# Loading a weight matrix in four row groups per slice, so that its casts need no change of partition

## The chip, the cores and the metric

The kernel runs on one core of a Trainium2 chip. The metric is device time in microseconds (us), the median of the runs shown; lower is better. TensorE multiplies; VectorE (DVE), ScalarE (ACT) and GpSimd (POOL) work on tiles; SyncE (SP) issues most of the transfers, which 16 DMA engines carry out.

## The reference

A linear attention with cosine weights (8 batches, 8 heads, 576 positions, head size 64) feeds a two-layer network with 4608 tokens, model width 512 and inner width 2048:

```python
def phi(x, c, s):
    r = np.maximum(x, 0.0)
    return np.concatenate([r * c, r * s], axis=-1)
q_p, k_p = phi(q, cos_w, sin_w), phi(k, cos_w, sin_w)
kv = np.einsum('bhsf,bhsd->bhfd', k_p, v)
z = np.sum(k_p, axis=2)
num = np.einsum('bhsf,bhfd->bhsd', q_p, kv)
den = np.einsum('bhsf,bhf->bhs', q_p, z)[..., None] + 1e-06
x = (num / den).transpose(0, 2, 1, 3).reshape(B * S, H * D)
h = x @ w_in
g = h * (1.0 / (1.0 + np.exp(-beta * h)))
out = g @ w_out
```

Inputs and output are float32; the kernel multiplies in bfloat16.

## The kernel before, in words

The tokens are taken in nine chunks of 512. For each batch the kernel applies the relu to q and k (L193, L192), scales v by cosine and sine (L219, L217), forms kv (`kv_mm`, L276), the numerators and denominators (`num_mm`, L297), divides (L308 to L319), and turns the result so that the model dimension lies on the partitions (`x_turn_pe`, L356, or a transposing transfer, L367). A chunk then goes through w_in in 16 groups of four matmuls of 128x512 (`h_mm`, L386), each followed by the activation (L394), and through w_out (`o_mm`, L544, for the first chunk; later chunks use a scheme with fewer products, L511 and L621). The order on each engine is the order in which the program text issues the instructions; there is no scheduler behind it.

Heads are paired on the partitions in an order of their own: in the turned x, partition jj*64 + d of block (jp, g) holds dimension d of head jp*4 + jj*2 + g. The rows of w_in must stand in the same order. w_in is loaded in four slices of 512 columns. `load_w("in", i)` (L95 to L103) reads slice i into a float32 stage tile of 128 partitions x 4 x 512: partition q of block j holds row j*128 + q. `cast_win` (L105) then makes the bfloat16 tile `win[i]`, and since rows of the two halves of the partitions have to change places, it works on pieces of 64 partitions. For one (g, jj) it reads partitions g*64 onward and writes partitions jj*64 onward:

```python
o = win[i].rearrange("q (jp g) f -> q jp g f", g=2)[jj * HP : (jj + 1) * HP, jps, g, f0:f1]
a = stages["in", i].rearrange("q (jp jj) f -> q jp jj f", jj=2)[g * HP : (g + 1) * HP, jps, jj, f0:f1]
```

Slice 0 is loaded in two transfers of 512 KB, right behind the first batch's q, k and v; slices 1 to 3 in one transfer of 1 MB each. Slice 0 is cast in eight pieces of 64x512 (five on GpSimd, two on VectorE, one on ScalarE), slice 1 in eight pieces of 64x2x256 on VectorE, slices 2 and 3 likewise with two of the eight on GpSimd (L113 GpSimd, L115 VectorE, L111 ScalarE).

There are four stage tiles. The four slices of w_out (`load_w("out", i)`, L101) reuse those of w_in, so each of these transfers waits until the casts of the slice before it in its tile are done. Behind the second of them on SP's queue stand the next batch's v, k and q (L79). VectorE and ScalarE scale w_out on its way to bfloat16 (L123, L121). The program gives the transfers of SP and ScalarE eight semaphores in turn, so that a transfer waits until the eighth before it has landed.

The part of the program around the change runs in this order: kv and numerators of the first batch's two head groups, casts of slice 0, division and turning of the second group, `cast_halves(1)`, then the slots of the first chunk (0 to 3 on slice 0, 4 to 7 on slice 1, and so on; 16 to 31 for w_out). `rest()` is issued at slot 4: casts of slices 2 and 3, the loads of w_out and of batch 1, scaling of w_out and the preparation of batch 1. Slots 22 and 23 issue batch 1's kv (L276) and the turning of its q (L235).

Of the kernel before, what the change touches and what calls it, by code (L numbers as in the profile page):

```python
# [16 lines left out]
P = 128  # L17
# [5 lines left out]
def kernel(  # L23
# [14 lines left out]
    nc = tc.nc  # L38
# [5 lines left out]
    MI = DM // P  # L44
# [4 lines left out]
    HP = P // 2  # L49
# [33 lines left out]
    win = [const.tile([P, MI, 512], BF16, name=f"win{i}") for i in range(4)]  # L83
# [4 lines left out]
    T1, T2, T4 = (const.tile([P, JT // 2, HM], BF16, name=f"T{i}") for i in (1, 2, 4))  # L88
    T3 = B12
    S1, S2, S3, S4 = (const.tile([P, JT // 2, TCH // 2], BF16, name=f"S{i}") for i in (1, 2, 3, 4))  # L90
    w_in_v = moe_w_in.rearrange("(j p) f -> p j f", p=P)
    w_out_v = moe_w_out.rearrange("(j p) m -> p j m", p=P)
    stages = {}

    def load_w(kind, i, step=4):  # L95
        if (kind, i) not in stages:
            stages[kind, i] = stage.tile([P, 4, 512], FP32, name="w_stage", tag="w_stage")
        st = stages[kind, i]
        for a in range(0, 4, step):
            if kind == "out":  # L100
                nc.sync.dma_start(out=st[:, a : a + step], in_=w_out_v[:, 4 * i + a : 4 * i + a + step, :])  # L101
                continue
            nc.sync.dma_start(out=st[:, a : a + step], in_=w_in_v[:, a : a + step, i * 512 : (i + 1) * 512])  # L103

    def cast_win(i, gj, eng="dve", f0=0, f1=512, jps=slice(0, 2)):  # L105

        g, jj = gj
        o = win[i].rearrange("q (jp g) f -> q jp g f", g=2)[jj * HP : (jj + 1) * HP, jps, g, f0:f1]
        a = stages["in", i].rearrange("q (jp jj) f -> q jp jj f", jj=2)[g * HP : (g + 1) * HP, jps, jj, f0:f1]
        if eng == "act":  # L110
            nc.scalar.copy(o, a)  # L111
        elif eng == "pool":
            nc.gpsimd.tensor_copy(o, a)  # L113
        else:
            nc.vector.tensor_copy(o, a)  # L115
# [7 lines left out]
            nc.vector.tensor_scalar(wout[:, j, :], st[:, jj, :],  # L123
                                    scalar1=rbeta[:, j : j + 1], scalar2=None, op0=ALU.mult)

    GJ = [(0, 0), (0, 1), (1, 0), (1, 1)]

    load_raw(0, "q", 0, 2)
    load_raw(0, "q", 2, 4)
# [5 lines left out]
    load_raw(0, "k", 2, 3)  # L135
    load_raw(0, "k", 3, 4)
    load_w("in", 0, 2)


# [150 lines left out]
    def num_mm(b, n, jp, bank, slot):  # L290

        for cs in range(2):
            for jj in range(2):
                rows = slice(jj * HP, (jj + 1) * HP)
                for g in range(2):
                    cols = slice(g * HP, (g + 1) * HP)
                    nc.tensor.matmul(  # L297
                        ps[cols, bank + jj, slot * E : (slot + 1) * E],
                        lhsT=(qts[b % 2], qs_of(b))[cs][rows, jp, n, cols],
                        rhs=kv[rows, g, jp, cs, :],  # L300
                        start=(cs == 0), stop=(cs == 1))

    def x_rden(bank, slot, n0, n1, jps):

        w, m = len(jps), n1 - n0
        nv = ps[:, bank : bank + 2, slot * E : (slot + w * m) * E].rearrange("q j (i s e) -> q j i s e", s=w, e=E)
        den = small.tile([P, 2, m, w], FP32, name="den", tag=f"den{m}{w}")
        nc.vector.tensor_tensor(  # L308
            den, nv[:, :, :, :, D],
            eps9[:, n0:n1].unsqueeze(1).unsqueeze(3).to_broadcast([P, 2, m, w]), op=ALU.add)  # L310
        rden = small.tile([P, 2, m, w], FP32, name="rden", tag=f"rden{m}{w}")
        nc.vector.reciprocal(rden, den)  # L312
        return nv, rden, n0, jps
# [409 lines left out]
    for i in range(1, 4):  # L723
        load_w("in", i)
# [14 lines left out]
    for n in range(7):  # L739
        num_mm(0, n, 1, 0, n)  # L740
    num_mm(0, 7, 1, 6, 0)
    for gj, eng in zip(GJ, ("pool", "dve", "pool", "dve")):
        cast_win(0, gj, eng, jps=slice(0, 1))
    for gj, eng in zip(GJ, ("act", "pool", "pool", "pool")):
        cast_win(0, gj, eng, jps=slice(1, 2))
    got = x_rden(0, 0, 0, 7, (1,))
    x_mul_act(x_rden(6, 0, 7, 8, (1,)), 7)
    x_mul(got, 0, 4)
# [4 lines left out]
    x_turn_pe(0, 4, 8, 1, ("act",), (1,))  # L753
    h_mm(0, 3, (0, 1))

    def cast_halves(i, fs=(0, 256)):
        for f in fs:
            for gj in GJ:
                cast_win(i, gj, "pool" if i > 1 and gj == GJ[3] else "dve", f, f + 256)

    cast_halves(1)

    def rest():

        cast_halves(2)
        cast_halves(3)
        x_mul(x_rden(2, 0, 8, NQ, (0, 1)), 8, NQ)
        load_w("out", 0)
        load_w("out", 1)
        load_raw(1, "v")  # L770
        load_raw(1, "k")
        load_raw(1, "q")
        load_w("out", 2, 2)
        load_w("out", 3, 2)
        x_turn_dma(0, 8, 9)
        for j in range(8):
            cast_out(j)
        v_scale(1, 0)
        v_scale(1, 1, n0=8)
        k_relu(1, 0, 2)  # L780
        q_relu(1, 0)
        q_relu(1, 1, n1=5)
# [309 lines left out]
```

## Time and profile before

| what | value |
|---|---|
| times of the runs | 273.31, 273.50, 275.48 us; median 273.5 us |
| span of the profiled execution | 272.7 us (0.8 below the median of the runs) |
| TensorE busy | 265.3 us, 97% of the span |
| VectorE busy | 224.0 us, 82% |
| ScalarE busy | 188.4 us, 69% |
| GpSimd busy | 68.3 us, 25% |
| HBM read, written | 36.71 MB, 9.44 MB |
| w_in's transfers | three of 1024 KB, 12.8 us from issue to landing; two of 512 KB, 10.8 us |

The time of the profiled execution itself is not listed apart from the runs; its span stands for it. "PE" is TensorE's matmul, "PEld" its weight load, "SPq" the transfers issued by SyncE. L12 is line 12 of the kernel. Idle time is given with what ended it ("<-DMA w_stage" means that the landing of that tile did). Times of day are counted from the start of the span. Matmuls overlap in the pipeline, so their shown durations are longer than their distance.

### The profile page before, as it was taken

The numbers are of one execution on the slowest core, as the hardware profiler recorded it, in microseconds if no ns is written. First come the engines' busy times: TensorE is split into PE (matmuls) and PEld (weight loads), VectorE is DVE, ScalarE is ACT, GpSimd is POOL, SyncE is SP. The second block draws the span as 40 slices with busy tenths as digits, with TensorE's granted clock in tenths as the row PEclk, the third lists the DMA queues.
The fourth block names the chain that finished last, engine by engine and source line by source line (L and its number), as shares of the span: only waits on it lengthen the run. The fifth ranks groups of instructions, "written<-read, shape, count | busy, mean of one in ns | idle before, by whom it ended". The sixth has DMA issues, their size and how long they took to land.

```text
span 272.7 us, 8970 instructions
## 1 busy us (share of the span) xinstructions
PE 265.3 (97%) x3712; PEld 206.8 (76%) x3712; DVE 224.0 (82%) x596; ACT 188.4 (69%) x384; POOL 68.3 (25%) x89
## 2 busy tenths in 40 slices
PE   8899999999899999999999999999999999999994
PEld 8554455455784588888888888888888888888883
DVE  5989969499989889789989997899589768757852
ACT  4778777796419656899489966996696179428920
POOL 1444000510078000660085009300840060000001
PEclk9999999999999999999999999999999999999999
DMA  6999999999969999994589439943600570015005
GB/s 237 374 395 383 392 390 319 379 201 336 284 130 311 240 348 226 240 313 103 147 216 370 92 58 223 332 71 62 181 2 2 61 185 1 2 27 130 0 2 155
DMA packets 50681, 54.00 MB, mean 198 GB/s; under 512 B 31232, under 2 KB 31760, under 8 KB 50640
## 3 DMA queue, kind: packets, MB, share of 16 engines
q1 hardware_dynamic: 47504, 45.55, 59.1%
q0 software_dynamic: 2784, 7.61, 9.6%
q8 instruction: 29, 0.48, 0.7%
q10 hardware_dynamic: 352, 0.27, 0.4%
q14 instruction: 12, 0.10, 0.1%
HBM read 36.71 MB, written 9.44 MB: 169 GB/s over the span
## 4 chain that ended last, share of the span: by engine, by line
PE 85%; DVE 9%; DMA 3%; SPq 1%; issue 1%; ACT 1%; DVEq 0%
PE ps L621 32%; PE ps L511 27%; PE ps L386 10%; PE ps L544 5%; PE ps L563 4%; PE ps L297 3%; DMA raw_v<-in_v_dram 3%; PE ps L276 3%; DVE vb L219 1%; DVE xs L319 1%; DVE qs L223 1%; SPq L79 1%; DVE S L406 1%; DVE rk L193 1%; DVE qb L193 0%
## 5 line engine op out<-in xcount | busy, mean ns | idle before, releaser
L537 POOL DMA_DIRECT2D out_dram<-o_sb x58 | 33.9, 591 | 147.3 <-ACT o_sb L658 86.3
L420 ACT ACTIVATE g_t<-ps,beta 128x512 bf16<-128x512 f32 x96 | 60.3, 702 | 1.4 <-PE ps L511 1.3
L621 PEld LDWEIGHTS <-S 128*128 128x128 bf16 x448 | 43.4, 98 | 5.2
L511 PE MATMUL ps<-w_stage 128*128 128x256 bf16 x288 | 46.6, 272 | 0.1
L386 PE MATMUL ps<-xt,win 128*128 128x512 bf16 (+1 forms) x196 | 42.8, 375 | 0.1
L511 PEld LDWEIGHTS <-w_stage 128*128 128x128 bf16 x384 | 37.3, 98 | 5.1 <-issue 0.2
L487 DVE TENSOR_TENSOR ps<-ps,p 128x256 f32<-128x256 f32 x74 | 30.5, 428 | 8.6 <-PE ps L511 3.0
L394 ACT ACTIVATE g_t<-ps,beta 128x512 bf16<-128x512 f32 x48 | 32.3, 688 | 7.2 <-PE ps L386 7.1
L621 PEld LDWEIGHTS <-g_t 128*128 128x128 bf16 x336 | 32.3, 98 | 4.5 <-ACT g_t L420 0.4
L386 PEld LDWEIGHTS <-win 128*128 128x128 bf16 x196 | 18.7, 98 | 21.1 <-issue 0.5
L511 PE MATMUL ps<-xt,win 128*128 128x256 bf16 x192 | 32.9, 273 | 0.0
L511 PEld LDWEIGHTS <-win 128*128 128x128 bf16 x288 | 28.0, 98 | 3.4
L621 PE MATMUL ps<-wout,g_t 128*128 128x256 bf16 x224 | 28.9, 273 | 0.0
L406 DVE TENSOR_TENSOR S<-g_t 128x512 bf16<-128x512 bf16 (+1 forms) x66 | 25.7, 418 | 3.3 <-ACT g_t L420 1.7
L480 ACT COPY ps<-ps 128x256 f32<-128x256 f32 x62 | 22.6, 383 | 7.5 <-PE ps L621 4.0
L217 ACT ACTIVATE vb<-raw_v,sin 128x256 bf16<-128x256 f32 (+1 forms) x58 | 26.0, 503 | 1.5 <-DMA raw_v<-in_v_dram 1.5
L621 PE MATMUL ps<-T,S 128*128 128x256 bf16 x224 | 26.6, 273 | 0.0
L621 PE MATMUL ps<-wout,S 128*128 128x256 bf16 x224 | 26.4, 273 | 0.0
L319 DVE TENSOR_TENSOR xs<-ps,rden 128x768 bf16<-128x768 f32 (+4 forms) x26 | 22.8, 884 | 0.9 <-DVE rden L312 0.2
L223 POOL TENSOR_TENSOR qs<-qt,tanr 128x1152 bf16<-128x1152 bf16 x6 | 14.3, 2387 | 27.4 <-PE ps L563 21.0
L658 ACT COPY o_sb<-ps 128x512 f32<-128x512 f32 x11 | 6.3, 587 | 20.1 <-PE ps L621 20.1
L487 DVE TENSOR_TENSOR ps<-ps,u 128x256 f32<-128x256 f32 x36 | 15.3, 427 | 5.3 <-PE ps L511 3.3
(112 smaller groups left out, 414.7 us busy)
## 6 DMA issues: line engine op xcount, KB each, us to landing
raw_v<-in_v_dram SPq DMA_DIRECT2D x7, 1152.0 KB, 9.7
raw_k<-in_k_dram SPq DMA_DIRECT2D x7, 1152.0 KB, 9.5
raw_q<-in_q_dram SPq DMA_DIRECT2D x7, 1152.0 KB, 7.4
out_dram<-o_sb POOLq DMA_DIRECT2D x58, 128.0 KB, 4.5
w_stage<-in_moe_w_in_dram SPq DMA_DIRECT2D x3, 1024.0 KB, 12.8
w_stage<-in_moe_w_out_dram SPq DMA_DIRECT2D x2, 1024.0 KB, 7.9
w_stage<-in_moe_w_out_dram SPq DMA_DIRECT2D x4, 512.0 KB, 11.9
out_dram<-o_sb SPq DMA_DIRECT2D x10, 128.0 KB, 2.4
```

The costliest lines, as they stand in the source:

```text
L217: got = nc.scalar.activation(o, a, AF.Copy, scale=t[:, n : n + 1])
L223: return eng.tensor_tensor(dst.rearrange("q n (g p) -> q n g p", g=2), src.rearrange("q n (g p) -> q n g p", g=2), tanr[:, n0:n1].unsqueez ...
L319: nc.vector.tensor_tensor(o.rearrange("q j n s d -> q j (n s) d"), nv[:, :, a:z, :, 0:D].rearrange("q j n s d -> q j (n s) d"), rden[:, :, ...
L386: nc.tensor.matmul(ps[:, h_bank(c, jt), i * 64 : (i + w) * 64], lhsT=win[jt // 4][:, mi, (jt % 4) * P : (jt % 4 + 1) * P], rhs=xt[:, i : i ...
L394: return nc.scalar.activation(gs[c, jt // 4][:, jt % 4], ps[:, h_bank(c, jt)], AF.Silu, scale=beta[:, jt : jt + 1])
L406: return nc.vector.tensor_tensor(o, l, r, op=op)
L420: return nc.scalar.activation(gs[c, jt // 4][:, jt % 4], bank, AF.Silu, scale=beta[:, jt : jt + 1])
L480: return nc.scalar.copy(at("a", 0), at("b", 0))
L487: nc.vector.tensor_tensor(dst, at("b", 0), st["p5"], op=ALU.add)
L511: nc.tensor.matmul(dst, lhsT=l[:, g], rhs=r[:, :, g * HP : (g + 1) * HP], start=start and g == 0, stop=g == 1, skip_group_check=True)
L537: (eng or own).dma_start(out=out_v[bb, n][:, m0:m1], in_=o_sb[hf * HP : (hf + 1) * HP, m0:m1])
L621: nc.tensor.matmul(dst, lhsT=l(i), rhs=r[:, i], start=start and i == 0, stop=i == order[-1], skip_group_check=True)
```

## The change

The view of w_in is split so that one transfer fetches, for a block (jp, g), the two groups of 64 rows that belong on the lower and the upper half of the partitions. A slice is now four transfers of 256 KB, one for each block, each into all 128 partitions. The stage then has the partition order of `win`, and a cast takes any set of blocks over all 128 partitions. Slice 0 is cast block by block (GpSimd, VectorE, ScalarE, GpSimd), slices 1 to 3 in two pieces of four blocks x 256 columns each, all on VectorE. The size of the stage, the bytes loaded and the places of the calls in the program stay.

```diff
-    w_in_v = moe_w_in.rearrange("(j p) f -> p j f", p=P)
+    w_in_v = moe_w_in.rearrange("(jp jj g d) f -> jp g jj d f", jp=2, jj=2, g=2)
...
+        if kind == "in":
+            for mi in range(MI):
+                nc.sync.dma_start(out=st[:, mi], in_=w_in_v[mi // 2, mi % 2, :, :, i * 512 : (i + 1) * 512])
+            return
         for a in range(0, 4, step):
-            if kind == "out":
-                nc.sync.dma_start(out=st[:, a : a + step], in_=w_out_v[:, 4 * i + a : 4 * i + a + step, :])
-                continue
-            nc.sync.dma_start(out=st[:, a : a + step], in_=w_in_v[:, a : a + step, i * 512 : (i + 1) * 512])
+            nc.sync.dma_start(out=st[:, a : a + step], in_=w_out_v[:, 4 * i + a : 4 * i + a + step, :])
...
-    def cast_win(i, gj, eng="dve", f0=0, f1=512, jps=slice(0, 2)):
-        g, jj = gj
-        o = win[i].rearrange("q (jp g) f -> q jp g f", g=2)[jj * HP : (jj + 1) * HP, jps, g, f0:f1]
-        a = stages["in", i].rearrange("q (jp jj) f -> q jp jj f", jj=2)[g * HP : (g + 1) * HP, jps, jj, f0:f1]
+    def cast_win(i, mis, eng="dve", f0=0, f1=512):
+        o, a = win[i][:, mis, f0:f1], stages["in", i][:, mis, f0:f1]
...
-    for gj, eng in zip(GJ, ("pool", "dve", "pool", "dve")):
-        cast_win(0, gj, eng, jps=slice(0, 1))
-    for gj, eng in zip(GJ, ("act", "pool", "pool", "pool")):
-        cast_win(0, gj, eng, jps=slice(1, 2))
+    for mi, eng in enumerate(("pool", "dve", "act", "pool")):
+        cast_win(0, slice(mi, mi + 1), eng)
...
-    def cast_halves(i, fs=(0, 256)):
-        for f in fs:
-            for gj in GJ:
-                cast_win(i, gj, "pool" if i > 1 and gj == GJ[3] else "dve", f, f + 256)
+    def cast_halves(i):
+        for f in (0, 256):
+            cast_win(i, slice(0, MI), "dve", f, f + 256)
```

More of the change, by code (lines that the diff above doesn't have):

```diff
@@ L124, in cast_out @@
                                     scalar1=rbeta[:, j : j + 1], scalar2=None, op0=ALU.mult)
-    GJ = [(0, 0), (0, 1), (1, 0), (1, 1)]
     load_raw(0, "q", 0, 2)
```

## Prediction

> **What bounds the kernel now.** I read the page's first parts, then the chain that ended last in order of time, then the timelines of GpSimd, VectorE, ScalarE and TensorE up to 62 us, and the busy time by windows. In the chain the columns are start, length, engine and line.
>
> ```profile
> PE 265.3 (97%) x3712; PEld 206.8 (76%) x3712; DVE 224.0 (82%) x596; ACT 188.4 (69%) x384; POOL 68.3 (25%) x89
> 3.16 9.06 DMA raw_v<-in_v_dram
> 12.25 0.92 DVE vb L209
> ...
> 15.65 0.42 DVE win L115
> 16.08 0.03 issue
> 16.11 0.72 DVE win L115
> 16.83 0.03 issue
> 16.86 0.19 DVE den L308
> ...
> 19.04 3.03 PE ps L386 x18
> 22.07 0.25 PE ps L297 x16
> 22.33 9.60 PE ps L386 x44
> 31.93 6.04 PE ps L544 x28
> 37.97 1.15 PE ps L276 x72
> 39.12 0.97 PE ps L544 x4
> 40.09 1.07 PE ps L235 x18
> ```
>
> The reader is to see three things. Two casts of w_in (L115) stand on the chain. From 19.04 us on TensorE works without a hole through the stretch that consumes w_in (L386), w_out (L544) and the next batch's keys and queries (L276, L235). The whole program is 97% TensorE, so any wait of TensorE there is paid in full. The second view says what feeds that stretch (start, length, and in brackets the idle time before and what ended it).
>
> ```profile
> 15.09 3.54 POOL L113 CAST win<-w_stage 64x512 bf16<-64x512 f32 x5 [1.54 <-DMA w_stage<-in_moe_w_in_dram]
> 21.87 1.55 POOL L113 CAST win<-w_stage 64x512 bf16<-64x512 f32 x2 [3.24 <-DMA w_stage<-in_moe_w_in_dram]
> 24.56 1.36 POOL L113 CAST win<-w_stage 64x512 bf16<-64x512 f32 x2 [1.14 <-DMA w_stage<-in_moe_w_in_dram]
> 19.11 10.23 DVE L115 CAST win<-w_stage 64x512 bf16<-64x512 f32 x20 [0.52 <-DMA w_stage<-in_moe_w_in_dram]
> 39.17 1.16 DVE L193 TENSOR_SCALAR qb<-raw_q 128x1152 bf16<-128x1152 f32 x2 [2.25 <-DMA raw_q<-in_q_dram]
> 33.20 3.31 ACT L217 ACTIVATE vb<-raw_v,sin 128x256 bf16<-128x256 f32 x8 [0.55 <-DMA raw_v<-in_v_dram]
> 36.41 1.15 ACT L192 ACTIVATE rk<-raw_k 128x1152 bf16<-128x1152 f32 x1
> 37.90 1.22 PE L276 MATMUL ps<-vb,rk 64*64 64x130 bf16 x72
> 14.00:24.50 10.50, 10.12 (x168) 5.65 (x168) 9.57 (x23) 8.32 (x19) 4.87 (x7) 1.00 1.05 391
> 24.50:36.00 11.50, 11.50 (x55) 5.15 (x54) 11.17 (x31) 9.37 (x17) 1.36 (x2) 1.00 1.05 390
> ```
>
> In the two window rows the last columns are granted clock 1.00, DMA share 1.05 and 391 and 390 GB/s: the DMA engines are full from 14 to 36 us, and every load lands in the order of one stream. Slices 1, 2 and 3 of w_in end waits at 19.11, 21.87 and 24.56, some 2.7 us per MB. Behind them raw_v ends a wait at 33.20 and raw_q one at 39.17. Both are just in time. ScalarE's keys end at 36.41 + 1.15 = 37.56, and TensorE wants them at 37.90. VectorE's first half of the queries ends at 39.17 + 0.58 = 39.75, and TensorE wants it at 40.09. The slack is 0.34 us in both places. So the stretch is bound by TensorE with the load stream a third of a microsecond behind it: a later stream is paid almost whole, and an earlier VectorE buys nothing.
>
> **The change part by part.** *Casts.* Slice 0 goes from eight pieces of 64 partitions to four of 128, the later slices from eight pieces each to two of 128x1024. GpSimd loses seven of nine casts, VectorE goes from 22 to 7.
>
> ```profile
> 30.12 3.25 DVE L123 TENSOR_SCALAR wout<-w_stage,rbeta 128x512 bf16<-128x512 f32 x8
> ```
>
> The wide VectorE cast lies between 1024/1152 of the 0.58 us of L193, 0.52, and two casts of 128x512 at 0.41 (this row), 0.82; I take 0.65. Slice 1 then costs 1.3 instead of 8 x 0.42 = 3.4, slices 2 and 3 1.3 instead of 2.5 each, and slice 0 0.42 instead of 1.18: some 5.3 us less VectorE. On the path it is worth little. L308 at 16.86 also waits for TensorE's last numerators (L297, the next fence), at 16.51 + 0.21 = 16.72, so the 0.76 us saved in slice 0 shrink to about 0.1. The rest ends in the 2.25 us that VectorE already idles for raw_q. I count 0.1 us, and at worst nothing. GpSimd's pieces keep 512 elements a partition (3.54/5 = 0.71 us); twice that would still end before 18.66, when the stage is given on now. What is new is that VectorE's first cast of a slice waits for all four transfers, and everything behind it on VectorE (L308, L319, w_out's scaling L123) waits too; that costs nothing while slices land as now.
>
> ```profile
> 16.51 0.21 PE L297 MATMUL ps<-kv,qs 64*64 64x65 bf16 x4
> 18.66 4.68 SPq L101 DMA_DIRECT2D w_stage<-in_moe_w_out_dram  x2
> 4.66 8.30 SPq L103 DMA_DIRECT2D w_stage<-in_moe_w_in_dram  x5
> ```
>
> *Issues.* SP issues 16 transfers of 256 KB instead of 5. The five took 8.30 us, to 12.96, and SP then waits until 18.66; eleven more at the half microsecond of an issue fit there. In the program each transfer waits for the eighth before it, which keeps about 2 MB queued: no gap in the stream.
>
> *The shape of the transfers.* This term decides. Each old load has 128 rows as the first level on both sides: 128 partitions, and under each some rows of 2 KB. A new one reads rows jj*128 + d, which do not merge into one level: its source stays 2 x 64 x 512, and the built program carries it so, against 128 x 1 x 512 in SBUF. No row shows such a transfer. What rows show is how a transfer is shared out.
>
> ```profile
> q1 hardware_dynamic: 47504, 45.55, 59.1%
> q10 hardware_dynamic: 352, 0.27, 0.4%
> out_dram<-o_sb ACTq DMA_DIRECT2D x4, 64.0 KB, 2.5
> beta<-in_moe_beta_dram ACTq DMA_DIRECT2D x1, 8.0 KB, 2.6
> ```
>
> ScalarE's queue (q10) carries five transfers: four of 64 rows and beta's 16 rows make 272 packets. The other 80 are 16 for each transfer, one per DMA engine. So even 8 KB of 16 rows went one row to each engine: the cut is made along the first level, and every first level in this kernel (16, 64, 128) gives 16 equal shares. A first level of two gives two. I bound the term by all 16 engines (a slice in 2.7 us, no cost) and by two (eight times that), and take two, because the cut that q10's row shows has nothing else to cut in the source. The Trainium skill's page "DMA: Bandwidth & Descriptors", section "Why a DMA increments its semaphore by 16 and not by 1", states this as a rule: the number of engines is the largest, up to 16, that divides the slowest dimension of both sides, so 2 and 128 give 2. q10's 352 packets agree with it for 16 and 64 rows. By that rule the sum is the one below, and without it the first rival's; no run here shows a transfer on fewer than 16 engines.
>
> *The sum.* An engine moves 390/16 = 24.4 GB/s, so two move a slice of 1.05 MB in 21.5 us and the four in 86.0. The stream of w_in begins at about 24.56 - 4 x 2.69 = 13.8, and slice 3 lands at 99.8 instead of 24.56: 75.2 us later. Everything behind it has a sixteenth of its bytes on those two engines, in order, so w_out, raw_v, raw_k and raw_q follow at the same distances as now, all 75.2 later, and TensorE's 37.97 and 40.09 move by 75.2 - 0.34. The casts' 0.1 has no place to count. TensorE's restart after idling is an unknown: the rows here show its clock at 1.00 throughout. Its first use of slice 3 lies some 28.4 us in (four groups of 9.60/11 = 0.87 before w_out's 31.93), so 9.5 us of work stand between it and L276 at 37.97. In the new times that is 100.5 (99.8 and a cast of 0.65) to 112.9, 12.4 us. At half speed the work would take 9.5 longer, of which 2.9 are free; I take nothing and keep 6.6 for the range. The span becomes 272.7 + 74.9 = 347.6. The median of the runs (273.5) lies 0.8 above the span: 348.4 us.
>
> ```profile
> 7.00:8.00 1.00, 1.00 (x9) 0.80 (x8) 0.96 (x3) 0.54 (x2) 0.00 (x0) 1.00 1.00 350
> 48.00:49.00 1.00, 1.00 (x11) 0.69 (x10) 0.17 (x1) 0.48 (x1) 0.00 (x0) 1.00 1.12 408
> ```
>
> The rate of two engines is bounded by the slowest and fastest full microseconds: 350/16 = 21.9 GB/s makes 95.8 us of the four slices and a time of 358; 408/16 = 25.5 makes 82.2 and 344.6. Two engines alone may be faster than any sixteen together; as an estimate I allow the same 8% again that lies between 379, the middle of the two rows, and its ends: 75.6 us, time 338.
>
> **The rivals.** *All 16 engines take part* (not slower; also the case in which the change's cost is nil). For it: nothing in the trace shows a transfer on fewer, and the bytes are the same. Against it: q10's cut. Then slices land as now, the four quarters of slice 0 a little sooner, the gain is the 0.1 us above, and eleven more transfers may cost the stream a few tenths against a slack of 0.34: 273.4 us, from 272.8 to 275.
>
> *VectorE's time is the bound after all* (faster). If the 5.3 us of shorter casts came off the end, the time would be 268.2. For it: two casts stand on the chain. Against it: TensorE has no hole from 19.04 on, and VectorE waits for raw_q, not for its own work. It decides only if raw_q landed over 2.25 us sooner.
>
> **How the numbers follow.** Two engines 0.84: the cut along the first level is shown three ways (16, 64, 128 rows), and a first level of two leaves it no third piece. Sixteen engines 0.14, faster through VectorE 0.02. The predicted time is the first case's, 348.4, its range 338 to 358 by the bounds of the rate; it leaves out the other two cases, 0.16. A measurement of this kernel can tell about 1% (2.7 us) from no change. Slower by more comes from the first case and a sliver of the second, 0.85; within 1% 0.13; faster 0.02.
>
> **What would show it.** If right: DMA share near 0.125 and 49 GB/s from some 15 to 100 us; w_in's casts released by DMA about 21.5 us apart; queue q1 with 47504 - 5 x 16 + 16 x 2 = 47456 packets (with 16 engines 47680); TensorE idle in four long holes before 100 us, and from L276 on the old distances. What would make it wrong: w_in landing at 24 to 25 us (the first step falls), holes of other length (the rate), or holes behind 115 us (the restart, or loads that do not follow in order).

## The result, and the profile after

| | before | after |
|---|---|---|
| median of the runs compared | 273.86 us (273.31 to 275.48) | 352.38 us (350.95 to 354.49) |
| ratio | | 1.286, 95% interval 1.281 to 1.291 |
| profiled execution: span | 272.7 us | 348.8 us, time 350.95 us |
| mean granted clock | 1.00 | 0.90 |

The changed kernel takes 1.29 times as long. 348.4 us was predicted, from 338 to 358. The profile page of the changed kernel answers to the lines shown before as follows (busy time and share of the span of each engine; the granted clock, DMA share in tenths and GB/s in 40 slices of 8.7 us; the queue of SP's transfers with packets, MB and share; the group of the later slices' multiplications with its idle time and what ended most of it; the group of VectorE's casts).

```profile
PE 274.5 (79%) x3708; PEld 208.6 (60%) x3712; DVE 218.0 (63%) x581; ACT 188.8 (54%) x384; POOL 63.3 (18%) x82
PEclk9975556758569999999999999999999999999999
DMA  7411111111998899989999928935973205302304
GB/s 268 178 50 52 50 50 51 50 50 56 283 360 271 213 294 223 327 156 311 309 198 285 268 51 248 340 77 125 306 85 86 79 5 82 108 3 53 69 2 120
q1 hardware_dynamic: 47456, 45.55, 48.1%
L384 PE MATMUL ps<-xt,win 128*128 128x512 bf16 (+1 forms) x196 | 52.4, 429 | 60.2 <-DVE win L114 55.4
L114 DVE CAST win<-w_stage 128x1024 bf16<-128x1024 f32 (+1 forms) x7 | 4.3, 653 | 78.2 <-DMA w_stage<-in_moe_w_in_dram 78.2
```

The reader is to see the eight slices at 50 to 56 GB/s with a DMA digit of 1: the transfers that had filled 16 engines now keep an eighth of them busy. q1 has exactly the 47456 packets that two engines a transfer were predicted to give. TensorE waits 55.4 us for VectorE's casts of w_in, and VectorE 78.2 us for their loads. VectorE itself is free; a wait named after an engine has to be followed one step further.

The timelines of GpSimd, VectorE and ScalarE give the landings (start, length, and in brackets the idle time before and what ended it). The first four are the four blocks of slice 0, the last three slices 1 to 3.

```profile
17.16 0.61 POOL L112 CAST win<-w_stage 128x512 bf16<-128x512 f32 x1 [3.91 <-DMA w_stage<-in_moe_w_in_dram]
22.33 0.43 DVE L114 CAST win<-w_stage 128x512 bf16<-128x512 f32 x1 [7.00 <-DMA w_stage<-in_moe_w_in_dram]
27.54 0.62 ACT L110 CAST win<-w_stage 128x512 bf16<-128x512 f32 x1 [11.08 <-DMA w_stage<-in_moe_w_in_dram]
32.77 0.61 POOL L112 CAST win<-w_stage 128x512 bf16<-128x512 f32 x1 [15.00 <-DMA w_stage<-in_moe_w_in_dram]
53.66 1.29 DVE L114 CAST win<-w_stage 128x1024 bf16<-128x1024 f32 x2 [29.27 <-DMA w_stage<-in_moe_w_in_dram]
74.47 1.29 DVE L114 CAST win<-w_stage 128x1024 bf16<-128x1024 f32 x2 [19.52 <-DMA w_stage<-in_moe_w_in_dram]
98.19 1.30 DVE L114 CAST win<-w_stage 128x1024 bf16<-128x1024 f32 x2 [22.42 <-DMA w_stage<-in_moe_w_in_dram]
```

SP's queue in the same timeline, and three rows of the busy time by windows (the five engines, then granted clock, DMA share and GB/s):

```profile
4.59 76.52 SPq L101 DMA_DIRECT2D w_stage<-in_moe_w_in_dram  x16
```

```profile
14.00:24.50 10.50, 4.40 (x115) 2.38 (x115) 3.30 (x10) 2.07 (x6) 0.61 (x1) 0.83 0.14 52
36.00:58.00 22.00, 4.41 (x26) 1.32 (x25) 1.29 (x2) 2.06 (x3) 0.00 (x0) 0.50 0.13 50
80.00:100.00 20.00, 1.75 (x7) 0.53 (x5) 1.74 (x5) 1.24 (x2) 0.00 (x0) 0.65 0.71 214
```

Blocks land 5.2 us apart, slices 20.9, 20.8 and 23.7. The SP row says that 16 issues took 76.52 us, 4.8 each: SP's queue is held back until the engines take more. In the window rows the share is 0.13 to 0.14 at 50 to 52 GB/s as long as w_in is alone. The last row takes in the loads of w_out and batch 1's inputs, which SP issued from 81.30 on and which moved beside w_in from 86 on (0.71, 214).

The chain that ended last shows where the lost time is paid. Of the fourteen SPq pieces, which follow one another from 6.37 to 81.1, the first and the last are quoted.

```profile
6.37 7.50 SPq L101
...
76.04 5.07 SPq L101
81.30 32.82 DMA w_stage<-in_moe_w_out_dram x2
114.68 1.89 PE ps L542 x8
118.30 1.81 issue
...
145.45 10.59 PE ps L561 x96
...
242.12 11.21 PE ps L509 x100
```

The corresponding pieces of the kernel before are 41.16 (L544), 70.15 (L563) and 166.88 (L511). They now come 73.5, 75.3 and 75.2 later, and the span ends 76.1 later. All but about 1 us is lost before 121 us.

### The profile page after: what moved, and what is told of

Its sections match the earlier page's. It is cut to its first block, busy times and chain, and to the rows that moved or that the text cites. A ratio compares the mean times of both kernels' runs of the same rounds, so it can differ in the third digit from the quotient of the medians.

```text
span 348.8 us, 8956 instructions
## 1 busy us (share of the span) xinstructions
PE 274.5 (79%) x3708; PEld 208.6 (60%) x3712; DVE 218.0 (63%) x581; ACT 188.8 (54%) x384; POOL 63.3 (18%) x82
## 3 DMA queue, kind: packets, MB, share of 16 engines
q1 hardware_dynamic: 47456, 45.55, 48.1%
## 4 chain that ended last, share of the span: by engine, by line
PE 65%; SPq 21%; DMA 11%; issue 1%; DVE 0%
PE ps L619 25%; PE ps L509 21%; SPq L101 21%; DMA w_stage<-in_moe_w_out_dram 9%; PE ps L384 8%; PE ps L561 4%; PE ps L295 3%; PE ps L542 2%; PE ps L274 2%; DMA raw_q<-in_q_dram 1%; PE ps L354 0%; DVE wout L122 0%; SPq L79 0%; DVE o_sb L650 0%; SPq L104 0%
## 5 line engine op out<-in xcount | busy, mean ns | idle before, releaser
L384 PE MATMUL ps<-xt,win 128*128 128x512 bf16 (+1 forms) x196 | 52.4, 429 | 60.2 <-DVE win L114 55.4
L384 PEld LDWEIGHTS <-win 128*128 128x128 bf16 x196 | 20.5, 109 | 88.3 <-DVE win L114 57.6
L114 DVE CAST win<-w_stage 128x1024 bf16<-128x1024 f32 (+1 forms) x7 | 4.3, 653 | 78.2 <-DMA w_stage<-in_moe_w_in_dram 78.2
L509 PEld LDWEIGHTS <-win 128*128 128x128 bf16 x288 | 28.0, 98 | 3.4
L217 DVE TENSOR_SCALAR vb<-raw_v,cos 128x256 bf16<-128x256 f32 x63 | 19.8, 364 | 1.3 <-DMA raw_v<-in_v_dram 1.3
```

The source lines that it names most:

```text
L384: nc.tensor.matmul(ps[:, h_bank(c, jt), i * 64 : (i + w) * 64], lhsT=win[jt // 4][:, mi, (jt % 4) * P : (jt % 4 + 1) * P], rhs=xt[:, i : i ...
L509: nc.tensor.matmul(dst, lhsT=l[:, g], rhs=r[:, :, g * HP : (g + 1) * HP], start=start and g == 0, stop=g == 1, skip_group_check=True)
```

## The experiments

Ten kernels ran, each timed beside the kernel before on the same chip. Diffs are against the changed kernel unless they say otherwise; in them `...` stands for lines left out, and `cols` is short for `i * 512 : (i + 1) * 512`.

### 4, 8 and 16 pieces as the first level

```diff
-    w_in_v = moe_w_in.rearrange("(jp jj g d) f -> jp g jj d f", jp=2, jj=2, g=2)
+    w_in_v = moe_w_in.rearrange("(c g d) f -> g c d f", c=C, g=4)   # C = 4, 8, 16
...
-  in_=w_in_v[mi // 2, mi % 2, :, :, cols]
+  in_=w_in_v[mi, :, :, cols]
```

Four pieces:

> Changed part: each of the 16 transfers reads four groups of 32 rows instead of two of 64 (first level 4), so the rows stand in another order on the partitions and the network's product is not the reference's; bytes, number of transfers, casts and order of work are those of the changed kernel. Theory (the cut falls along the first level): four engines at the 25.6 GB/s an engine that the changed kernel shows (256 KB in 5.11 us on two) take 40.9 us for w_in instead of 81.8; slice 3 lands near 55 us, the time is 304 us (302 to 308), and the page's first queue carries 47456 + 32 = 47488 packets. Rival 1 (SP needs 5 us to issue one such three-level transfer, and 16 issues are the bound): unchanged, near 352 us. Rival 2 (256 KB is too small a transfer): unchanged, near 352 us.

Eight pieces:

> Changed part: first level 8 (eight groups of 16 rows), otherwise as the run with first level 4; the product is again not the reference's. Theory: eight engines take 20.5 us for w_in, slice 3 lands near 34.5 us, time 284 us (282 to 287), 47552 packets on the first queue. Both rivals (slow issue, small transfer): near 352 us.

Sixteen pieces:

> Changed part: first level 16 (sixteen groups of 8 rows), again with the rows in another order and a product that is not the reference's. Theory: all 16 engines, slice 3 lands at 24 to 25 us, time within 1% of the kernel before (273 to 275 us), 47680 packets on the first queue. Both rivals (slow issue, small transfer): near 352 us, since the transfers have the same size, number and three levels as in the changed kernel. A middle outcome, 276 to 280 us, would say that sixteen small transfers cost something of their own.

Number of transfers (16), their size (256 KB) and the casts are the same in all of these and in the changed kernel. The "casts of slice 3" are the begin of VectorE's, which a load releases; the rate and the DMA share are those of the window from 14 to 24.5 us.

| first level | us | q1 packets | GB/s | DMA share | SP's 16 issues | casts of slice 3 |
|---|---|---|---|---|---|---|
| 2 (changed kernel) | 352.4 | 47456 | 52 | 0.14 | 76.52 | 98.19 |
| 4 | 313.4 (one run) | 47488 | 103 | 0.27 | 39.38 | 58.77 |
| 8 | 290.9 (one run) | 47552 | 205 | 0.54 | 20.32 | 38.29 |
| 16 | 281.4 (ratio 1.025, 1.019 to 1.030) | 47680 | 287 | 1.06 | 18.78 | 30.39 |

Without the 16 packets that each of its five loads of w_in adds, the kernel before has 47504 - 5 x 16 = 47424 packets in q1. Every row here is 47424 and 16 x its first level, one more packet for each transfer and engine. So the first level is the number of engines. Up to eight the rate doubles from row to row (205/8 = 25.6 GB/s an engine), and SP's issues shrink with it. That decides against transfers that are slow because they are small, or issues that are slow by themselves: both would have left all four at 352. The rule of the Trainium skill that the prediction named (page "DMA: Bandwidth & Descriptors", section "Why a DMA increments its semaphore by 16 and not by 1") holds here for 2, 4, 8 and 16.

The times of the rows with four and eight pieces lie above what was expected (302 to 308 and 282 to 287). In both, the casts of slice 3 begin 3.8 us later than expected (58.77 against 55, 38.29 against 34.5): the last slice took 14.0 us after one of 10.4, and 8.3 after 5.9, with w_out's loads issued behind it (at 43.90 and 25.39), as in the changed kernel. TensorE's waits also list 3.1 and 3.3 us of holes with no releaser. Where the rest comes from is open.

The last row fell short too. 273 to 275 was expected, and 276 to 280 if something else was in it; it was 281. Its engines are all busy (share 1.06) but move 287 GB/s where the kernel before moves 391. Read straight from the trace's packets of that window, a 2 KB packet took 118 ns (median) against 86 before. So a second effect exists, which the runs by pieces and by halves below take apart.

### Four pieces of 64 partitions a slice

```diff
-    w_in_v = moe_w_in.rearrange("(jp jj g d) f -> jp g jj d f", jp=2, jj=2, g=2)
+    w_in_v = moe_w_in.rearrange("(jp jj g d) f -> g jj d jp f", jp=2, jj=2, g=2)
...
-            for mi in range(MI):
-                nc.sync.dma_start(out=st[:, mi], in_=w_in_v[mi // 2, mi % 2, :, :, cols])
+            for n in range(4):
+                g, jj = divmod(n, 2)
+                nc.sync.dma_start(out=st[jj * HP:(jj + 1) * HP, g::2], in_=w_in_v[g, jj, :, :, cols])
```

> The reference's product, with the wide casts kept: each of a slice's four transfers of 256 KB fills 64 partitions of two blocks instead of 128 partitions of one, so the first level is 64 on both sides; number and size of transfers as in the changed kernel. Theory: 16 engines, and the time is that of the kernel before within 1% (273 to 275.5 us). A rival of another kind, that a transfer into only 64 partitions writes at half the rate: w_in takes 21 us instead of 10.5 and the time is near 284 us. Slow issue or small transfers: near 352 us.

282.89 us, ratio 1.034 (1.030 to 1.038). q1 has 47680 packets and the share is 1.06, so 16 engines take part, but they move 235 GB/s and a packet takes 146 ns. The row of the busy time by windows:

```profile
14.00:24.50 10.50, 7.44 (x126) 4.12 (x126) 4.11 (x15) 5.03 (x13) 1.51 (x3) 0.67 1.06 235
```

This is the rival's outcome. The product is the reference's, the casts are wide, and 69 of the 78 us that the change lost are back; still it is slower than the kernel before.

### The casts alone, and with 16 transfers

The diff is against the kernel before: its five loads stay, and the casts are those of the change, in the same numbers and on the same engines. In the second run `load_w("in", i, 1)` makes 16 transfers of 256 KB of the loads, still with 128 rows as the first level.

```diff
-    def cast_win(i, gj, eng="dve", f0=0, f1=512, jps=slice(0, 2)):
...
+    def cast_win(i, mis, eng="dve", f0=0, f1=512):
+        o, a = win[i][:, mis, f0:f1], stages["in", i][:, mis, f0:f1]
```

> The loads of the kernel before (five transfers, 128 partitions as the first level on both sides) with the changed kernel's wide casts; the rows of w_in then stand in another order, so the product is not the reference's, while every instruction's size is that of the changed kernel. Theory (the casts lie beside other work; VectorE waits for the queries behind them): busy time of VectorE about 5 us less, slices landing as before, time within 0.3 us of the kernel before, a ratio of 0.998 to 1.001. Rival (VectorE's time is the bound): 268 us, a ratio of 0.981.

> As the run of the casts alone, but with 16 transfers of 256 KB, each of 128 rows as the first level on both sides (the rows of w_in again in another order). Number and size of the transfers are those of the changed kernel, the shape is that of the kernel before. If the loss that was left with 16 engines (281 us) came from eleven more transfers or their size: about 280 us and under 300 GB/s. If it came from which partitions each engine writes: 380 to 390 GB/s from 14 to 24 us, 2 KB packets near 84 ns, q1 with 47680 packets, 273.5 to 274.5 us. By the other explanation of the changed kernel, that small transfers are slow in themselves, 352 us.

The casts alone took 275.66 us, ratio 1.007 (1.004 to 1.010); with 16 transfers it was 276.64, ratio 1.011 (1.009 to 1.012). The first misses its theory by 1.8 us on the slow side, and its rival by 7.7. VectorE did become shorter, as its timeline in the run of the casts alone shows, and then idles for the next landing:

```profile
19.48 1.30 DVE L113 CAST win<-w_stage 128x1024 bf16<-128x1024 f32 x2 [0.69 <-DMA w_stage<-in_moe_w_in_dram]
22.18 1.29 DVE L113 CAST win<-w_stage 128x1024 bf16<-128x1024 f32 x2 [1.40 <-DMA w_stage<-in_moe_w_in_dram]
24.88 1.30 DVE L113 CAST win<-w_stage 128x1024 bf16<-128x1024 f32 x2 [1.41 <-DMA w_stage<-in_moe_w_in_dram]
39.27 1.16 DVE L190 TENSOR_SCALAR qb<-raw_q 128x1152 bf16<-128x1152 f32 x2 [2.26 <-DMA raw_q<-in_q_dram]
```

The wait for raw_q ends at 39.27, against 39.17 before: 5 to 6 us less VectorE moved nothing. Part of the loss can be seen in the waits of TensorE, which list two of 1.2 us together (total, times, longest), put down to "issue" (nothing that the profile shows), a line that the kernel before does not have:

```profile
PE ps L294 <- issue: 1.2, 2, 0.7
```

These two holes are not the whole loss. The two profiled executions differ by only 0.2 us in span (272.9 and 272.7), while the medians of the runs differ by 1.5 (273.6 and 272.1). Followed matmul by matmul, the first hole (0.52 us at 68.93) is made up at once, because the kernel before waits 0.96 us just behind that place (L563 at 70.15; here the same piece begins at 69.87). The second (0.67 at 179.58) leaves TensorE some 0.6 us later. Where the rest of the loss lies is not shown.

The second run settles the number of transfers, though its time lies 2.1 us above the 274.5 at most that was expected. Its window row from 14 to 24.5 us ends in 1.04 and 367, that from 24.5 to 36 in 1.05 and 391 (share, GB/s), with packets of 84 ns. Splitting the loads costs 1.0 us over the casts alone: the queries begin at 39.84 instead of 39.27 in VectorE's timeline, and TensorE waits 0.7 us for them. That is the slack of 0.34 us at work. But its profiled execution also has holes of 2.5 us put down to "issue", against 1.2 in the casts alone, so the 1.0 us cannot be put down to the landings alone. It is not what separates 16 pieces (281) from 128 rows (277).

### The casts alone, with as many instructions as before

```diff
+    scrap = {e: const.tile([HP, 8], BF16, name=f"scrap_{e}") for e in ("dve", "pool")}
+    def pad(i, n, eng="dve"):
+        for _ in range(n):
+            (nc.gpsimd if eng == "pool" else nc.vector).tensor_copy(scrap[eng], stages["in", i][0:HP, 0, 0:8])
```

> The run of the casts alone with 15 casts of 64x8 elements on VectorE and 7 on GpSimd added behind the wide ones, into a scrap tile, so that each engine has as many instructions as in the kernel before; the rows of w_in are again in another order. The casts alone cost 1.8 us; 0.3 of them lie outside the span (2.1 us instead of 1.8) and 1.2 in two holes of TensorE that nothing in the profile released. If these come from how the program's code falls on its loading (its length per engine): 273.4 to 274.2 us, 1.8 us outside the span, no such holes. If the wide casts cost by themselves, by what they release sooner: 275.4 to 276.2 us, holes as before.

275.05 us, ratio 1.004 (1.003 to 1.006): between the two. The time outside the span fell from 2.1 to 1.8 us, but the holes stayed. They are in the waits of TensorE and in the chain:

```profile
PE ps L300 <- issue: 1.6, 2, 1.4
```

```profile
179.37 1.36 issue
```

So with the wide casts the span stays 1.4 us longer (273.3 against 271.9 in the median), and padding does not take that away. In the run of the casts alone the hole lies at 179.58 (0.67). In the packets of the traces an instruction packet of 16 KB (of the queue with 29 of them, taken for TensorE's, which has 7424 of the 8970 instructions) came late just there: fetched from 175.8 to 176.8 in the kernel before, from 175.5 to 179.0 in the casts alone and from 177.5 to 178.6 in the padded run, in a stretch where a transposing transfer of SP's queue and batch loads overlap. Other traces fit: with 16 pieces, with 32 pieces and with 16 transfers a packet of 3.3 to 3.8 us ends 0.4 to 0.8 us before the hole. The version by halves and its variant with two queues have the same wide casts and neither a late packet nor a hole at that place, so wide casts by themselves do not make the hole. That the late instructions make it is argued from this coincidence, not shown. Nor is the time outside the span settled: the version by halves has 1.8 us without padding.

### Which partitions 16 engines write

```diff
+    w_in_v = moe_w_in.rearrange("(c g d) f -> g c d f", c=32, g=4)
```

> The changed kernel with 32 pieces of four rows as the first level instead of two of 64 (the rows of w_in in another order). Sixteen engines take part, q1 has 47680 packets, as with 16 pieces of eight rows (281 us, 287 GB/s, packets of 118 ns). If each engine takes two neighbouring pieces, it writes the same eight adjacent partitions as there: 281 us, 287 GB/s. If it takes two pieces that lie 32 partitions apart: 380 to 390 GB/s, packets of 84 ns and 276 to 277 us, as with 128 rows as the first level.

276.88 us (one run), 47680 packets. The row of the busy time by windows from 14 to 24.5 us for 16 pieces of eight rows, and then the one for 32 pieces of four:

```profile
14.00:24.50 10.50, 7.42 (x140) 4.31 (x140) 5.77 (x17) 7.82 (x17) 1.52 (x3) 1.00 1.06 287
```

```profile
14.00:24.50 10.50, 10.09 (x168) 5.71 (x169) 6.03 (x15) 8.32 (x18) 1.23 (x2) 1.00 1.05 384
```

287 became 384 GB/s, and the packet 86 ns again, at the same size, number and engines. Only the division of the rows differs: a piece is eight adjacent partitions in the first and four in the second. The run ends where 128 rows ended (276.6). So the 4 to 5 us of the 16 pieces are the price of how the rows are divided, most likely of which partitions are written at one time. The division also changes which rows are read from HBM at one time, and no run separates the two; nor does the profile show which pieces an engine took.

For the 64 partitions, the blocks of the changed kernel were cut into two transfers each (first run), and the upper halves of the version by halves were given to ScalarE's queue (second):

```diff
+                for jj in range(2):
+                    nc.sync.dma_start(out=st[jj * HP:(jj + 1) * HP, mi], in_=w_in_v[mi // 2, mi % 2, jj, :, cols])
```

```diff
-                nc.sync.dma_start(out=st[jj * HP:(jj + 1) * HP, g::2],
+                (nc.sync, nc.scalar)[jj].dma_start(out=st[jj * HP:(jj + 1) * HP, g::2],
```

> Each block of the changed kernel in two transfers of 64 rows, one into the lower and one into the upper 64 partitions: 32 transfers of 128 KB, two levels on both sides, the product is the reference's. If writing into 64 partitions at a time is what slowed the version by halves (283 us): 235 to 270 GB/s, packets of 145 ns, 282 to 285 us. If its three-level pattern did that: 380 GB/s, 273.5 to 275.5 us. If the number of transfers costs by itself, SP needs 16 more issues of half a microsecond, which lie before slice 3 is needed, 0 to 3 us.

> The version by halves (283 us: four transfers a slice, each 64 partitions x two blocks; the product is the reference's), with the transfers to the upper 64 partitions issued by ScalarE instead of SP, so that a lower and an upper half can be under way together. If an engine's packets last 146 ns because 16 engines write into half of the partitions at a time: packets fall to 84 to 100 ns and the rate to 340 to 390 GB/s where both queues run; the time is then 274 to 278 us, with up to some us added by the eight issues on ScalarE. If two such transfers take turns (the Trainium skill, page SBUF - State Buffer, measured only 6% more from two transfers at partitions 0 and 64 together): about 250 GB/s and 280 to 284 us.

The 32 transfers took 287.98 us, ratio 1.052 (1.049 to 1.054), outside what either theory expected, and for a reason of its own. The row of SP in the timeline and the row of the window say it (start and length of 32 issues; share and GB/s at the end):

```profile
4.63 28.42 SPq L102 DMA_DIRECT2D w_stage<-in_moe_w_in_dram  x32
```

```profile
14.00:24.50 10.50, 6.72 (x137) 4.04 (x136) 4.69 (x15) 8.02 (x18) 1.82 (x3) 1.00 0.53 169
```

The first eight issues are spread from 4.63 to 15.88 us, waiting for earlier loads to land. From 16.39 on SP issues without a pause: 0.60 us for an issue (the median), 0.70 from one to the next on the mean, and 128 KB each 0.70 us is 187 GB/s. The engines idle half the time, so packets seldom meet (median 84 ns). Only from 13 to 14 us, when transfers had queued up, were the engines full (share 1.01): 226 GB/s and packets of 141 ns, as the first theory had them. One microsecond is thin evidence on the 64 partitions.

The two queues took 287.12 us, ratio 1.049 (1.046 to 1.051), though not for the reason in either expectation. ScalarE issued six of its eight transfers only from 17.42 us on, for 8.40 us, and TensorE waited 7.6 us for ScalarE's next work (xs, L329). So from 14 to 22 us only lower halves were under way and from 27 to 31 us only upper ones, which makes it a measurement of one half at a time. The window row:

```profile
14.00:24.50 10.50, 2.59 (x102) 1.51 (x98) 3.83 (x9) 2.38 (x6) 2.74 (x3) 0.81 1.06 211
```

16 busy engines (1.06) move 211 GB/s (208 from 14 to 22 us alone), and a 2 KB packet takes 168 ns, twice the 84 to 86 of a write to all partitions; the upper half alone measured 169 to 171. From 23 to 26 us both queues had packets under way. The rate was 232 GB/s there, with medians of 139 to 161 ns, which is nearer to the second expectation (250 GB/s) than to the first (340 to 390). The Trainium skill, page "SBUF — State Buffer", section "Door 1: The DMA port swizzle (why `[64,N]` ≈ `[32,N]`)", gives half of the 16 ports for 64 partitions, some 218 GB/s, and the trace agrees with 211. In each microsecond from 23 to 26 most packets came from one queue, so whether two halves evenly mixed would bring the full rate was not measured.

## Why the prediction was right, point by point

**Shape of the transfers (two engines).** Right, and shown: packets, share and rate of the changed kernel, and the series 2, 4, 8, 16. q10's 352 packets had pointed to it. What the row did not show is that the same rule has a second half: 16 engines need not be full speed. The rival "all 16 engines" (273.4 us) fails: its 47680 packets come only with another first level, and even then the time is 277 at best (32 pieces, or 128 rows in 16 transfers) and 281 to 283 with the other divisions.

**Rate.** Mis-sized. 24.4 GB/s an engine was taken from the full stream; two engines alone moved 256 KB in 5.2 us (the distance of the landings; the issues in the chain are 5.07 to 5.09 long and some 5.12 apart), 25.2 GB/s an engine. That is 3% faster, as the allowance of 8% had left room for, and makes 20.8 us a slice instead of 21.5. It was hidden by the last slice: 23.7, because w_out and batch 1's inputs, on all engines, now ran beside it, issued from 81.30 on. In the trace the 2 KB packets of SP's queue (w_in's, and then w_out's too) took 84 ns until 88 us, 107 to 124 from 89 to 98, then 88 (medians of single microseconds). The prediction had them follow "in order" behind w_in; they overtook it on fourteen idle engines, and that step of the prediction was wrong. From the first block to slice 3 the stream took 86.2 us (12.0 to 98.19, the start being 17.16 - 5.2), against 86.0: two errors of some 2.9 us that cancel, which is luck. The start was 1.8 sooner than 13.8, so slice 3's casts began at 98.19 instead of 99.8, 73.6 us later than before.

**What follows slice 3.** Mostly as predicted, in another order. VectorE's and TensorE's queries in the timelines:

```profile
112.07 1.16 DVE L191 TENSOR_SCALAR qb<-raw_q 128x1152 bf16<-128x1152 f32 x2 [2.15 <-DMA raw_q<-in_q_dram]
112.89 1.18 PE L233 MATMUL ps<-ident,qb 128*128 128x128 bf16 x18 [0.24 <-DVE qb L191]
114.68 1.89 PE L542 MATMUL ps<-wout,g_t 128*128 128x512 bf16 x8 [0.62 <-DVE wout L122]
```

The queries are 72.9 later (39.17 to 112.07), 2.0 less than the 74.9 of the sum. Then TensorE waits 0.6 us for a part of w_out that had not been late (L542 behind the casts L122), which makes 73.5, and stands 1.81 us at 118.30 and 0.62 at 255.17 with no releaser, which makes about 76 of the 76.1. (A third hole, 0.72 at 144.32, costs nothing: it falls where the kernel before waits too, and the distance behind it is still 75.3.) These holes are a term that the sum did not have, and a hole behind 115 us was among the signs that the prediction gave for being wrong. The runs of the casts alone have their like, and in the changed kernel such a 16 KB packet took 7.06 us from 111.7 on, instead of about 1. So the mechanism, two engines, was right; that the span came within 1.2 us of the sum is in part luck, 2.0 us too much against some 3 us left out.

**Restart.** Half speed is real (granted clock 0.50 from 36 to 58 us, and the 16 products behind slice 3 took 5.55 us instead of 4 x 0.87), but all of it fitted into the waits for loads. The sum, which counted nothing for it, was right in that.

**Issues.** Hidden as said: with 128 rows as the first level, 16 transfers cost 1.0 us over five, and at least part of that goes with later landings (the queries 0.57 us later). In the changed kernel SP is on the chain for 21% of the span, but as the messenger of two full engines.

**Casts.** The duration was right (0.65 a wide cast, group mean 0.653; VectorE's busy time fell by 6.0 us, 5.3 said). Its worth of 0.1 us was wrong in sign: the casts alone cost 1.8 us (ratio 1.004 to 1.010), of which 0.3 lie outside the span. Of the 1.5 inside it, the profiled execution shows one hole of TensorE that leaves 0.6 us; the rest is open. "At worst nothing" was the step that failed here: the bound should have let in a loss.

**From span to time.** The 0.8 us between span and median came from two executions; in the later runs of the kernel before it is 1.8 us within one execution, and 2.15 in the changed kernel. This and the spread of the runs (350.95 was the profiled one, 352.38 the median) make most of the 4 us between forecast and median.

## What to carry to other kernels

Before reshaping a transfer, write down the first level of both sides as the instruction carries it: it sets how many DMA engines work (two levels of 64 rows that do not merge are two engines), and the trace confirms it from the packet count of the queue. Then ask which partitions those engines write at one time: 64 partitions ran at half rate and pieces of eight adjacent partitions at three quarters, with every engine fully busy. And price the gain first: casts beside a saturated load stream were worth nothing here, so no layout of the load could have paid for them in this program.

## What the runs showed of the hardware that was not expected

- A full DMA share does not mean full rate: at 1.05 to 1.06 the engines moved 391, 287, 235 and 211 GB/s, with 2 KB packets of 86, 118, 146 and 168 ns. GB/s beside the share tells it.
- Two to eight engines alone ran at some 25 GB/s each (256 KB in 5.2 us on two; 205 GB/s on eight, a little other traffic included), 16 together at 24.4.
- The profile lists the fetching of instructions as a DMA queue (q8: 29 packets, 0.48 MB). A 16 KB packet mostly takes about 1 us, but at times 3.3 to 7 us, and holes of 0.6 to 2.0 us without a releaser lie close behind. A change far away moved them about. That these packets cause the holes is not shown.
- SP took 0.60 us to issue a transfer of 128 KB and began one every 0.70 us; 16 engines were busy for 0.5 to 0.6 of the time.
